# Moving a third of a transform stage: fewer half transforms beside a sort, more in its drain, twelve behind it

## The chip, the cores and the metric

The kernel runs on one core of one Trainium2 chip. The metric is the time on the device in microseconds, the median of the runs shown. Engines are called by the names in the profile: PE (TensorE, with PEld for its weight loads), DVE (VectorE), ACT (ScalarE), POOL (GpSimd) and SP (SyncE, which here only issues DMAs).

## The reference, cut to what matters

Eight sequences of 5,696 tokens with 128 channels are convolved along time with one long filter per channel, and the result goes through a mixture of eight experts, of which each token takes the one with the highest gate.

```python
Xf = np.fft.rfft(x, n=2 * S, axis=1)              # x: (8, 5696, 128)
Hf = np.fft.rfft(h, n=2 * S, axis=0)
y = np.fft.irfft(Xf * Hf[None], n=2 * S, axis=1)[:, :S, :]
t = y.reshape(B * S, D)
logits = t @ w_gate                                # (45568, 8)
e = argmax(logits); g = softmax(logits)[e]
out = g * (np.maximum(t @ w1[e], 0) @ w2[e])       # w1: 128x1024, w2: 1024x128
```

## The kernel before, in words

The long convolution is done as a transform of two factors. The eight sequences are three groups of 2, 3 and 3. A group passes three stages. **Phase a** (`steps_a`) cuts the sequence into items: `xt` (120 x 512 floats) is loaded, cut into a rounded part and a remainder (`xc`, one cast on ACT and one subtraction), and two *half transforms* `pa` are made of it (cosine and sine, three matmuls of 512 columns each), copied into `ut` (the cosine half by ACT, the sine half by DVE) and, when three items have filled a `ut`, stored to U in DRAM. The second group (g = 1) has 36 items, so 72 half transforms and 24 stores of 737 KB. **Phase b** (`phase_b`) takes 120 *48-point items*: `uq` holds four of them, read from all rows of U; `xp` is the forward matmul, DVE multiplies by the filter (`zt`, `xs`), a *combine* adds the two, and `vp` is the inverse matmul. Since `uq` reads every row block of U, its load waits for the last U store. **Phase c** (`phase_c`) is the sort: synthesis `yp`, a transpose `tp`, gate scores `gb`, then small operations on DVE (`route`, `rank`) that give each token its place, and POOL scatters the rows to SR by those positions, six scatters per unit of six blocks. After a group's sort, `tables` computes on DVE, in pieces, which expert each tile of 256 rows belongs to.

**The experts** (`experts`) load the weights `wb` and the rows `xr` of a tile, turn the rows (`mx`), and run two layers (`mh`, `ma`) of 24 matmuls each. A tile's `xr` waits for all scatters of its sort, and its `wb` for the tables, whose values SP reads into registers.

What runs beside what is settled when the program is built. `run` mixes several streams by a virtual clock: each stream yields a cost, which is divided by its share, and the one that is furthest behind goes next. All engines then work through their own queue in that order. While the first sort runs (space "c"), the second group's phase a and the cutting of the weights go beside it. Then the space "sb" is opened, and `run((experts(), 1.0), (back, SHARES[3]))` mixes the experts with `rest()`, which runs phases b and c of the second and third groups. The experts yield `None` and stand still until their part is *ready*; `begin(pt)` makes it so, after the rest of the tables' pieces are issued. In `rest()` two pieces are dealt out per 48-point item, and `begin` comes when more than `HEAD[g]` of cost has been spent, 5500 for the second group, at 704 per item.

A `Guest` is a phase a that is stepped by hand inside another stage; the third group's runs so within the second sort.

SP's queue is one list in order. Every DMA on it waits for the semaphore lane of the DMA eight places ahead, so at most eight are under way.

Of the kernel before, what the change touches and what calls it, by code (L numbers as in the profile page):

```python
# [13 lines left out]
F32 = mybir.dt.float32  # L14
F32R = mybir.dt.float32r
# [11 lines left out]
MP = 120  # L27
# [10 lines left out]
SIX = 4  # L38
MT = 4
# [6 lines left out]
F3 = (False, False, True, False)  # L46
MIX = 2
LD = 4
SHARES = (0.42, 0.195, 0, 0.75, 0.998, 0.42)
GAP = 5000  # L50
AHEAD = 2
ALONE = (0, 14, 10)
HEAD = (0, 5500, 9000)
A3 = (True, True, True, True)
ALO = ('gpsimd', 'vector', 'vector', 'vector')
AT = 650
# [15 lines left out]
def conv_moe(ctx: ExitStack, tc: tile.TileContext, I, out, B, S, D, E, F, split):  # L72
    nc = tc.nc
    P = 128
# [14 lines left out]
    ps = pool("ps", 2, PSUM)  # L89
# [15 lines left out]
    sb = Space()  # L105
# [6 lines left out]
    class Part:  # L112
        def __init__(self, gr, s, b0, nb, c0, tiles):
            self.gr, self.g, self.s, self.b0, self.nb, self.c0 = gr, gr.g, s, b0, nb, c0
            self.cols = nb * D
            self.ni = SLOTS[gr.g] // nb
            while NB % self.ni:
                self.ni -= 1
            self.ns = self.ni * nb
            self.cb = 3 if self.ns % 3 == 0 else 2  # L120
            self.cw = self.cb * D
            self.c3 = C3[gr.g]
            self.nt = tiles
            self.ready = False
            self.ends = []
            self.sets = 2 if b0 + nb == B else 1
# [138 lines left out]
        while late:  # L265
            nc.sync.dma_start(*late.pop(0))

    def steps_a(gr, tag, bufs):
        g, nb = gr.g, gr.nb
        srcs = [(I["x"][gr.b0 + b], b) for b in range(nb)]  # L270
        tw = 4 * D
        items = []
        for ig in range(NB // 4):
            for src, b in srcs:
                items.append((ig, src, b))
        xts, uts, xss = {}, {}, {}
        fore = (4, 3, 2)[g]
        split = A3[g]

        def cut(n):  # L280
            if not split or n >= len(items):
                return
            xt = xts.pop(n)
            xs = sb.tile([MP, 2, tw], F32R, tag="us", name=f"xc{g}_{n}", bufs=3 if g else 2)
            nc.scalar.copy(xs[:, 0], xt)
            getattr(nc, ALO[g]).tensor_tensor(out=xs[:, 1], in0=xt, in1=xs[:, 0].bitcast(F32), op=ALU.subtract)  # L286
            xss[n] = xs

        def load(n):
            if n >= len(items):  # L290
                return
            ig, src, b = items[n]
            xts[n] = sb.tile([MP, tw], F32, tag="xt", name=f"xt{g}_{n}", bufs=1 + fore)
            nc.sync.dma_start(xts[n], src[:, ig * tw : (ig + 1) * tw])

        banks, late = {}, []

        def flush():
            while late:
                nc.sync.dma_start(*late.pop(0))  # L300

        def transform(m):
            n, c = divmod(m, 2)
            banks[m] = ps.tile([P, 512], F32, tag="cx", name=f"pa{g}_{n}_{c}", bufs=4)
            ops = [(fcs[:, c], xts[n])] if not split else [(fcr[:, u, c], xss[n][:, v]) for u, v in PASSES]
            for k, (lhs, rhs) in enumerate(ops):
                mm(banks[m][:QN, :], lhs, rhs, start=(k == 0), stop=(k == len(ops) - 1))
            if c == 1:
                (xss if split else xts).pop(n)

        def store(m):
            n, c = divmod(m, 2)
            ig, src, b = items[n]
            if b == 0:
                uts[c] = sb.tile([QN, 4, gr.cols], F32, tag=tag, name=f"ut{g}_{ig}_{c}", bufs=bufs)
            srcv = banks.pop(m)[:QN, :].rearrange("p (i d) -> p i d", d=D)
            lo = c * NB + ig * 4
            cp = nc.scalar.copy if c == 0 else nc.vector.tensor_copy
            cp(uts[c][:, :, b * D : (b + 1) * D], srcv)  # L319
            if b == nb - 1:  # L320
                late.append((gr.U[:, lo : lo + 4, :], uts[c]))

        def start():
            for n in range(fore):
                load(n)

        def begin(m):
            if m == 0:
                cut(0)
            if m % 2 == 0:  # L330
                load(m // 2 + fore)
                cut(m // 2 + 1)
            transform(m)

        return start, begin, store, flush, 2 * len(items)

    def phase_a(gr):
        start, begin, store, flush, M = steps_a(gr, "six", SIX - gr.g)
        half = AT if gr.g == 0 else 750 * RATE[3 * gr.g - 3]
        start()  # L340
        for m in range(M + 2):
            if m < M:
                begin(m)
            if gr.g == 0 and m == M - 8:
                ahead_of_b()
            yield half
            flush()
            if 1 <= m <= M:
                store(m - 1)
        yield 0  # L350
        flush()

    class Guest:
        def __init__(self, gr):
            self.start, self.step, self.store, self.flush, self.M = steps_a(gr, "mt", MT)
            self.gr, self.m, self.open = gr, 0, []

        def begin(self, count):
# [367 lines left out]
    def phase_c(pt, guest=None):  # L726
# [202 lines left out]
        for n in range(n_end + 1):  # L929
            for k in range(nsub):  # L930
                at = n * nsub + k
                if k == (1 if n == 0 else 0):
                    load(n + 2)
                if n < nu:
                    synth(n, k)
                if TL <= at < total_sub + TL:
                    tp = ps.tile([P, 512], F32, tag=ytag, name=f"tp{g}_{n}_{k}", bufs=ybuf)
                    turn(*divmod(at - TL, nsub), tp)
                if k == nsub - 1 and n >= 1:
                    score(n - 1, n - 2 if g else None)  # L940
                if k == 0 and n >= (n_end if g else 2):
                    if g:
                        yield STEP
                    score(None, n - 2)
                lift(at + 2)
                if guest:
                    guest.begin(1 if k == nsub - 1 and n >= 1 else 2)
                yield cost if n < nu or pt is parts[-1] else cost / 2
                if guest:
                    guest.end()  # L950
                if n < nu:
                    divide(*divmod(at + AHEAD, nsub))
                    settle(n, k)
                lifted(at + 2)
                if 0 <= at - TL < total_sub:
                    turned(*divmod(at - TL, nsub))
                chains = []
                if g and k == nsub - 1 and 0 <= n - 2 < nu:
                    chains.append(rank(n - 2))
                if k == nsub - 1 and 0 <= n - 1 < nu:  # L960
                    chains.append(route(n - 1))
                if k == 0 and n >= (n_end if g else 2):
                    chains.append(rank(n - 2))
                zipped(*chains)
                if n == n_end:
                    break
# [346 lines left out]
    def chain(*gens):  # L1313
        for x in gens:
            yield from x

    def rest():
        wait = [groups[0].parts[-1]]
        for gr in groups[1:]:
            spent = 0  # L1320
            guest = Guest(groups[gr.g + 1]) if gr.g + 1 < len(groups) else None
            bins = phase_b(gr)
            for n, cost in enumerate(bins):
                if guest and n == QN * gr.nch - 12:
                    guest.start()
                spent += cost
                yield cost
                if wait:
                    for _ in range(2):
                        next(wait[0].pieces, None)  # L1330
                    if spent > HEAD[gr.g]:
                        begin(wait.pop())
            for pt in gr.parts:
                yield from gather(pt, guest)
            if guest:
                yield from guest.rest()
                wait.append(gr.parts[-1])
# [26 lines left out]
    with tc.manual_schedule():  # L1364
        prep = weights()
        back = rest()
        run((phase_a(g0), 1.0), (phase_h(), SHARES[4]), (consts(), 1.0))
        sb.close()
        sb.open("b")
        state["rests"] = True  # L1370
        run((phase_b(g0), 1.0), (prep, SHARES[0]), stop=(prep,))
        sb.close()
        sb.open("c")
        state["rests"] = False
        run((chain(*[gather(pt) for pt in g0.parts]), 1.0), (phase_a(groups[1]), SHARES[1]), (prep, SHARES[5]))
        sb.close()
        sb.close()
        sb.open("sb")
        run((experts(), 1.0), (back, SHARES[3]))
        sb.close()  # L1380
# [78 lines left out]
```

## Time and profile before

| what | value |
|---|---|
| median of 3 runs | 2154.88 us (2150.51 to 2156.96) |
| the profiled execution's own time | 2172.09 us |
| its span, first to last instruction | 2170.2 us |
| mean granted TensorE clock | 0.981 |
| PE busy | 2082.0 us, 96% |
| DVE, POOL, ACT busy | 1543.0, 1351.6, 1187.0 us |
| phase c of the first group, roughly | 226 to 398 us |
| HBM read and written | 571 and 154 MB |

Busy time of PE counts matmuls that are running, at whichever clock is granted, so a stretch can be busy and slow. The span is that of one execution; the time shown for a run lies some 2 us above its span. Windows are in us from the span's start.

### The profile page before, as it was taken

Reading aid. Unit: us, or ns where it says so; the run is one execution under the profiler, and the core shown is the slowest. Engines: PE = TensorE matmul, PEld = TensorE weight load, DVE = VectorE, ACT = ScalarE, POOL = GpSimd, SP = SyncE. Lnnn points to the kernel's source line nnn. Section 1 sums busy time; section 2 is a strip of 40 time slices with the busy share of each in tenths; the row PEclk is TensorE's granted clock in tenths of the full one; section 3 lists DMA queues with packets and bytes.
Section 4 is the critical chain, followed back from the end, with each engine's and each line's share of the span. In section 5 each row is a group of like instructions: output and inputs, shape, how many; then the busy total and the mean of one; then the engine's idle time right before and its main releaser. Section 6 shows DMA issues by size and latency. Waiting matters only on the chain.

```text
span 2170.2 us, 47112 instructions
## 1 busy us (share of the span) xinstructions
PE 2082.0 (96%) x14452; PEld 1858.2 (86%) x14452; DVE 1543.0 (71%) x3373; ACT 1187.0 (55%) x2429; POOL 1351.6 (62%) x1569
## 2 busy tenths in 40 slices
PE   9999999799999999989999999999998999999998
PEld 7799777377777888878888889999988999999998
DVE  4698667799997777788888887666665555555554
ACT  5677555255555665636666665555544444445444
POOL 6566387545554488887997785288883444444333
PEclk9999999699999999999999999999999999999999
DMA  8899798989986898858777865656533334444331
GB/s 267 263 292 286 233 289 269 248 211 236 242 243 181 226 274 247 251 158 223 191 184 203 213 180 152 150 129 154 135 95 96 95 128 134 132 131 128 121 120 36
DMA packets 213409, 409.32 MB, mean 189 GB/s; under 512 B 31605, under 2 KB 135339, under 8 KB 213156
## 3 DMA queue, kind: packets, MB, share of 16 engines
q1 hardware_dynamic: 184975, 350.70, 57.7%
q0 software_dynamic: 27072, 55.35, 8.9%
q8 instruction: 117, 1.92, 0.4%
q14 instruction: 136, 1.11, 0.2%
q10 hardware_dynamic: 1109, 0.23, 0.1%
HBM read 571.44 MB, written 154.27 MB: 334 GB/s over the span
## 4 chain that ended last, share of the span: by engine, by line
PE 81%; DMA 6%; DVE 5%; issue 4%; POOL 2%; ACT 2%; SPq 1%; another core or an unknown queue 0%; POOLq 0%; ACTq 0%; DVEq 0%
PE mh L167 22%; PE ma L167 22%; PE vp L167 9%; PE xp L167 8%; PE yp L167 5%; PE mx L191 4%; PE pa L167 4%; PE gb L167 2%; DMA mt<-mq 2%; PE tp L191 1%; DMA wb<-WD 1%; DMA xt<-x 1%; PE lb L191 1%; PE hp L167 1%; POOL xc L286 1%
## 5 line engine op out<-in xcount | busy, mean ns | idle before, releaser
L1183 DVE SCALAR_TENSOR_TENSOR hs<-mh,hs 128x512 fp32r<-128x512 f32 x728 | 501.7, 690 | 393.5 <-ACT hs L1181 297.0
L167 PE MATMUL mh<-xtb,wb 128*128 128x256 f32 x4368 | 703.9, 297 | 20.9 <-DVE hs L1183 6.1
L1181 ACT ACTIVATE hs<-mh 128x512 fp32r<-128x512 f32 x728 | 435.4, 598 | 482.1 <-PE mh L167 375.0
L167 PEld LDWEIGHTS mh<-xtb,wb 128*128 128x128 f32 x4368 | 586.7, 190 | 91.0 <-issue 35.3
L167 PE MATMUL ma<-hs,wb 128*128 128x256 f32 x4368 | 656.4, 287 | 2.4 <-DMA wb<-WD 2.4
L167 PEld LDWEIGHTS ma<-hs,wb 128*128 128x128 f32 x4368 | 572.7, 191 | 3.8 <-DMA wb<-WD 3.3
L676 POOL DMA_INDIRECT SR<-rt,pi x384 | 408.5, 1064 | 206.1 <-ACT xtb L1165 85.4
L694 POOL DMA_INDIRECT out<-xr x308 | 302.7, 983 | 348.0 <-ACT hs L1181 160.7
L573 POOL TENSOR_TENSOR zt<-zt,xs 128x384 f32<-128x384 f32 (+1 forms) x276 | 295.8, 1074 | 154.7 <-DVE xs L563 72.7
L567 DVE TENSOR_TENSOR xs<-xp,hh 64x384 f32<-64x384 f32 (+1 forms) x360 | 214.8, 597 | 7.8
L610 ACT COPY vt<-vp 96x384 f32<-96x384 f32 x240 | 114.0, 475 | 191.7 <-PE vp L167 168.5
L167 PE MATMUL vp<-zt,mi 128*96 128x384 f32 x480 | 198.9, 496 | 1.7 <-issue 1.0
L558 DVE TENSOR_TENSOR zt<-xp,hh 128x384 f32<-128x384 f32 (+1 forms) x300 | 173.5, 578 | 24.9 <-PE xp L167 17.5
L167 PE MATMUL xp<-uq,mt 96*128 96x384 f32 (+1 forms) x496 | 174.7, 456 | 8.3 <-DMA uq<-U 4.4
L167 PE MATMUL pa<-xc,fcr 120*120 120x512 f32 x576 | 161.9, 416 | 4.2 <-DVE ut L319 1.2
L563 DVE SCALAR_TENSOR_TENSOR xs<-xp,hh 64x384 f32<-64x384 f32 x240 | 134.3, 560 | 4.2
L906 POOL MEMSET spent<- 120x288 f32 (+1 forms) x366 | 127.4, 348 | 0.5
L167 PEld LDWEIGHTS pa<-xc,fcr 120*120 120x120 f32 x576 | 101.1, 189 | 28.8 <-DVE rk L895 2.2
L167 PE MATMUL yp<-vr,gcr 120*120 120x384 f32 x576 | 118.8, 341 | 6.1 <-ACT ut L319 4.4
L167 PEld LDWEIGHTS vp<-zt,mi 128*96 128x96 f32 x480 | 78.9, 166 | 50.6 <-issue 27.1
L319 DVE COPY ut<-pa 120x512 f32<-120x512 f32 x96 | 65.7, 684 | 73.1 <-PE pa L167 47.9
L167 PEld LDWEIGHTS xp<-uq,mt 96*128 96x128 f32 x496 | 87.1, 199 | 32.5 <-issue 15.8
(165 smaller groups left out, 2754.6 us busy)
## 6 DMA issues: line engine op xcount, KB each, us to landing
wb<-WD SPq DMA_DIRECT2D x728, 512.0 KB
U<-ut SPq DMA_DIRECT2D x48, 720.0 KB
uq<-U SPq DMA_DIRECT2D x60, 576.0 KB
V<-vt SPq DMA_DIRECT2D x60, 576.0 KB
vq<-V SPq DMA_DIRECT2D x48, 720.0 KB
xt<-x SPq DMA_DIRECT2D x96, 240.0 KB
xr<-SR SPq DMA_DIRECT2D x154, 130.0 KB
WD<-wsp SPq DMA_DIRECT2D x32, 512.0 KB
```

Source lines behind the costliest of these rows:

```text
L167: nc.tensor.matmul(to, lhs, rhs, **kw)
L191: nc.tensor.transpose(dst, src, ident[:n, :n])
L558: nc.vector.tensor_tensor(out=zt, in0=x3, in1=hv[:, 0].broadcast_to([P, PK, cb, D]), op=ALU.mult)
L563: nc.vector.scalar_tensor_tensor(out=xs[to, 0], in0=x3[at, 0], scalar=-1.0, in1=him[:, 0], op0=ALU.mult, op1=ALU.mult)
L567: nc.vector.tensor_tensor(out=xs[to], in0=x3[at], in1=him, op=ALU.mult)
L573: eng.tensor_tensor(out=zt, in0=zt, in1=xs, op=ALU.add)
L610: done = nc.scalar.copy(outs_[qb][:, k0 : k0 + PK, c * cw : (c + 1) * cw], banks.pop(n)[:K2, :iw].rearrange("p (q x) -> p q x", q=PK),)
L676: s = nc.gpsimd.indirect_dma_start(out=SR[:, :], out_offset=IndirectOffsetOnAxis(ap=pi[:, b : b + 1], axis=0), in_=rt[:, b, :], in_offset= ...
L694: sc = nc.gpsimd.indirect_dma_start(out=out[:, :], out_offset=IndirectOffsetOnAxis(ap=xr[:, s, D + 1 : D + 2].bitcast(I32), axis=0), in_=x ...
L906: nc.gpsimd.memset(spent.rearrange("p c q -> p (c q)")[:, : REST[g]], 0.0)
L1181: done = nc.scalar.activation(hs[:, 0], hp, AF.Relu)
L1183: done = nc.vector.scalar_tensor_tensor(out=hs[:, 1], in0=hp, scalar=0.0, in1=hs[:, 0].bitcast(F32), op0=ALU.max, op1=ALU.subtract)
```

## The change

Five numbers and three pieces of code change. `SHARES[1]` falls from 0.195 to 0.132, so fewer half transforms go beside each step of the first sort. In the sort's drain (`n >= nu`, the steps after its last synthesis) the yielded cost is now twice a step's instead of half, so more go there. `phase_a(groups[1], LATE)` ends after 30 items; the last six items, twelve half transforms, become a `Guest` named `late` at the head of `rest()`, behind the first sort and in front of the second group's phase b, with two pieces of the tables dealt out at each of its steps. `HEAD[1]` becomes 0, so `begin` follows the first 48-point item, and with it the experts are let go there. `ALONE[1]` falls from 14 to 2: the combine of items 2 to 13 moves from DVE to POOL.

```diff
+LATE = 30
-SHARES = (0.42, 0.195, 0, 0.75, 0.998, 0.42)
+SHARES = (0.42, 0.132, 0, 0.75, 0.998, 0.42)
-ALONE = (0, 14, 10)
-HEAD = (0, 5500, 9000)
+ALONE = (0, 2, 10)
+HEAD = (0, 0, 9000)
...
-    def steps_a(gr, tag, bufs):
+    def steps_a(gr, tag, bufs, lo=0, hi=None, fore=None):
...
+        items = items[lo:hi]
...
-        fore = (4, 3, 2)[g]
+        fore = fore or (4, 3, 2)[g]
...
-    def phase_a(gr):
-        start, begin, store, flush, M = steps_a(gr, "six", SIX - gr.g)
+    def phase_a(gr, hi=None):
+        start, begin, store, flush, M = steps_a(gr, "six", SIX - gr.g, 0, hi)
...
-        def __init__(self, gr):
-            self.start, self.step, self.store, self.flush, self.M = steps_a(gr, "mt", MT)
+        def __init__(self, gr, lo=0):
+            self.start, self.step, self.store, self.flush, self.M = steps_a(gr, "mt", MT, lo, None, 2)
...
-                yield cost if n < nu or pt is parts[-1] else cost / 2
+                yield cost if n < nu or pt is parts[-1] else cost * (0.5 if g else 2)
...
         wait = [groups[0].parts[-1]]
+        late = Guest(groups[1], LATE)
+        late.start()
+        for cost in late.rest():
+            for _ in range(2):
+                next(wait[0].pieces, None)
+            yield cost
...
-        run((chain(*[gather(pt) for pt in g0.parts]), 1.0), (phase_a(groups[1]), SHARES[1]), (prep, SHARES[5]))
+        run((chain(*[gather(pt) for pt in g0.parts]), 1.0), (phase_a(groups[1], LATE), SHARES[1]), (prep, SHARES[5]))
```

What this does to PE's queue at the end of the first sort: `yp0_15_1` is the sort's last synthesis, `gb0_15` its last gate scores, `pa1_n_c` half c of item n of the second group, and `xp1_0` the first 48-point item. Before:

```order
L167 MATMUL yp0_15_1_4577<-hh1_109,spent_78 120x384 x2
L191 MATMUL tp0_15_1_4580<-ident_87,rt0_15_4540 128x120 x3
L167 MATMUL gb0_14_None_4584<-c_moe_w_gate_93,yt0_14_4511 120x8 x6
L191 MATMUL tp0_16_0_4610<-ident_87,rt0_15_4540 128x120 x3
...
L167 MATMUL gb0_15_None_4651<-c_moe_w_gate_93,yt0_15_4593 120x8 x6
...
L167 MATMUL xp1_0_0_4724<-uq1_0_4710,mt1_0_4708 128x384
```

Of the change:

```order
L168 MATMUL yp0_15_1_4420<-hh1_109,spent_78 120x384 x2
L192 MATMUL tp0_15_1_4423<-ident_87,rt0_15_4383 128x120 x3
L168 MATMUL gb0_14_None_4427<-c_moe_w_gate_93,yt0_14_4337 120x8 x6
L168 MATMUL pa1_26_0_4440<-xc1_26_4369,fcr_84 120x512 x3
...
L168 MATMUL pa1_26_1_4471<-xc1_26_4369,fcr_84 120x512 x3
L168 MATMUL pa1_27_0_4479<-xc1_27_4437,fcr_84 120x512 x3
...
L168 MATMUL gb0_15_None_4533<-c_moe_w_gate_93,yt0_15_4446 120x8 x6
L168 MATMUL pa1_28_1_4542<-xc1_28_4476,fcr_84 120x512 x3
L168 MATMUL pa1_29_0_4547<-xc1_29_4492,fcr_84 120x512 x3
L168 MATMUL pa1_29_1_4552<-xc1_29_4492,fcr_84 120x512 x3
...
L168 MATMUL pa1_30_0_4622<-xc1_30_4614,fcr_84 120x512 x3
...
L168 MATMUL pa1_35_1_4734<-xc1_35_4711,fcr_84 120x512 x3
L168 MATMUL xp1_0_0_4770<-uq1_0_4756,mt1_0_4754 128x384
```

Before, all 72 half transforms stood ahead of `yp0_15_1`; now 52 do, eight stand between it and the sort's end, and twelve (`pa1_30_0` to `pa1_35_1`) between the sort and `xp1_0`.

Further on in PE's queue, the first tile of the experts: `mxNone_0` turns its rows and `mh0_0` is its first matmul group. Before:

```order
L167 MATMUL xp1_9_0_4919<-uq1_8_4768,mt1_8_4735 128x384
L167 MATMUL vp1_5_0_4921<-zt1_5_0_4831,mi1_112 96x384
L167 MATMUL xp1_10_0_4931<-uq1_8_4768,mt1_8_4735 128x384
L167 MATMUL vp1_6_0_4933<-zt1_6_0_4848,mi1_112 96x384
L191 MATMUL mxNone_0_4953<-ident_87,xr0_4892 128x128 x2
L167 MATMUL mh0_0_4959<-xtb0_4956,wb0_0_0_4875 128x256 x6
```

Of the change:

```order
L168 MATMUL xp1_0_0_4770<-uq1_0_4756,mt1_0_4754 128x384
L168 MATMUL xp1_1_0_4774<-uq1_0_4756,mt1_0_4754 128x384
L168 MATMUL xp1_2_0_4831<-uq1_0_4756,mt1_0_4754 128x384
L168 MATMUL xp1_3_0_4844<-uq1_0_4756,mt1_0_4754 128x384
L192 MATMUL mxNone_0_4863<-ident_87,xr0_4807 128x128 x2
L168 MATMUL mh0_0_4869<-xtb0_4866,wb0_0_0_4790 128x256 x6
L168 MATMUL xp1_4_0_4876<-uq1_4_4764,mt1_4_4762 128x384
L168 MATMUL vp1_0_0_4878<-zt1_0_0_4777,mi0_111 96x384
```

Before, 11 `xp` and 7 `vp` were ahead of `mh0_0`; now 4 `xp` are. The experts stay about that much further ahead of the second and third groups' stages down to the last sort.

SP's queue over the same change of stage, from the last U stores to the first tile's rows `xr0`. Before:

```order
L300 DMA U1_72<-ut1_11_0_4378 120x1536
L300 DMA U1_72<-ut1_11_1_4425 120x1536
...
L461 DMA mt1_0_4708<-mq 96x512
L475 DMA uq1_0_4710<-U1_72 96x4x384
...
L475 DMA uq1_4_4718<-U1_72 96x4x384
...
L461 DMA mt1_8_4735<-mq 96x512
L475 DMA uq1_8_4768<-U1_72 96x4x384
...
L1144 DMA wb0_0_0_4875<-WD_77 128x1024
...
L1116 DMA xr0_4892<-SR_69 128x260
```

Of the change:

```order
L302 DMA U1_72<-ut1_9_1_4540 120x1536
L296 DMA xt1_30_4610<-x 120x512
...
L296 DMA xt1_35_4689<-x 120x512
...
L302 DMA U1_72<-ut1_11_0_4707 120x1536
L302 DMA U1_72<-ut1_11_1_4709 120x1536
L463 DMA mt1_0_4754<-mq 96x512
L477 DMA uq1_0_4756<-U1_72 96x4x384
...
L477 DMA uq1_4_4764<-U1_72 96x4x384
...
L463 DMA mt1_8_4772<-mq 96x512
...
L1146 DMA wb0_0_0_4790<-WD_77 128x1024
...
L1118 DMA xr0_4807<-SR_69 128x260
```

The weights `wb0` and rows `xr0` have moved up, from behind four `uq` loads to behind two; the U stores of items 30 to 35 and their loads now stand between the first sort and `uq1_0`.

## Rows read from the trace of the kernel before

**Rows 1.** The page, part 2: TensorE in 40 slices.

```profile
PE   9999999799999999989999999999998999999998
```

**Rows 2.** Windows: length, busy us (x) of PE, PEld, DVE, ACT, POOL; PEclk, DMA.

```profile
226.00:370.00 144.00, 138.84 (x737) 107.48 (x736) 95.80 (x276) 80.07 (x175) 90.84 (x133) 0.95 0.87 267
...
390.00:400.00 10.00, 3.67 (x20) 2.94 (x19) 6.23 (x31) 0.94 (x3) 8.71 (x15) 0.66 1.00 251
400.00:410.00 10.00, 7.13 (x12) 2.97 (x12) 7.74 (x24) 0.47 (x1) 8.58 (x14) 0.67 1.07 255
...
420.00:430.00 10.00, 8.46 (x12) 3.43 (x13) 9.57 (x18) 1.30 (x3) 0.00 (x0) 0.50 1.00 339
...
490.00:540.00 50.00, 50.00 (x277) 37.30 (x276) 47.02 (x87) 26.24 (x55) 28.50 (x30) 1.00 0.90 234
```

**Rows 3.** Windows of two later changes of stage.

```profile
940.00:990.00 50.00, 41.11 (x239) 34.28 (x240) 45.90 (x111) 18.40 (x39) 37.40 (x46) 0.90 0.72 196
1590.00:1640.00 50.00, 41.02 (x308) 38.93 (x307) 29.08 (x99) 17.14 (x38) 34.89 (x50) 0.93 0.24 67
```

**Rows 4.** Scatters of the first sort on GpSimd: one tile, then groups.

```profile
L676 POOL DMA_INDIRECT SR<-rt,pi x96: 995/999/1502, 257.4 to 415.2; - x96
...
L676 POOL DMA_INDIRECT SR<-rt,pi x96 | 100.4, 1046 | 58.8 <-DVE wsp L258 27.7 <-issue 14.7 <-ACT xc L285 6.5
L906 POOL MEMSET spent<- 120x224 f32 x90 | 27.8, 309 | 0.1
```

**Rows 5.** Timeline, first expert tile: start, us, engine, operation [idle, releaser].

```profile
418.43 0.15 DVE L1066 TENSOR_TENSOR did<-did,nt 1x8 f32<-1x8 f32 x1
...
430.12 0.63 PE L191 MATMUL mxNone<-ident,xr 128*128 128x128 f32 x2
...
431.21 1.32 PE L167 MATMUL mh<-xtb,wb 128*128 128x256 f32 x6 [0.46 <-ACT xtb L1165]
```

**Rows 6.** Chain of work, first sort: start, us, what.

```profile
363.35 2.07 PE pa L167 x9
...
369.38 1.29 PE yp L167 x4
```

**Rows 7.** Timeline, a stall in the first sort, and its end.

```profile
348.75 2.78 PE L167 MATMUL yp<-hh,spent 120*120 120x384 f32 x4 [2.45 <-ACT rt L813]
...
386.80 1.53 PE L167 MATMUL yp<-hh,spent 120*120 120x384 f32 x4
...
397.52 0.25 DVE L901 TENSOR_REDUCE pi<-rk 120x6 int32<-120x54 f32 x1
...
398.98 5.08 PE L167 MATMUL xp<-uq,mt 96*128 96x384 f32 x8 [2.69 <-DMA uq<-U]
```

**Rows 8.** Groups of VectorE and ScalarE in the first sort.

```profile
L286 DVE TENSOR_TENSOR xc<-xt,xc 120x512 fp32r<-120x512 f32 x36 | 24.7, 689 | 19.4 <-ACT xc L285 18.6 <-issue 0.5
L319 DVE COPY ut<-pa 120x512 f32<-120x512 f32 x36 | 24.5, 680 | 12.4 <-PE pa L167 6.9 <-issue 3.0 <-DMA U<-ut 2.5
...
L285 ACT CAST xc<-xt 120x512 fp32r<-120x512 f32 x36 | 22.5, 628 | 0.0
```

**Rows 9.** Chain of work, the very first load.

```profile
2.13 3.97 DMA xt<-x
```

**Rows 10.** Timeline of SP's queue over the change of stage.

```profile
380.60 4.70 SPq L300 DMA_DIRECT2D U<-ut  x2
...
390.37 1.22 SPq L475 DMA_DIRECT2D uq<-U  x1
...
400.66 0.32 SPq L461 DMA_DIRECT2D mt<-mq  x1
...
418.77 1.98 SPq L1144 DMA_DIRECT2D wb<-WD  x4
```

**Rows 11.** DMA over 340 to 440 us, in 40 slices.

```profile
GB/s 345 276 308 292 295 286 99 241 170 250 267 326 143 265 322 224 144 238 149 289 344 191 253 215 250 256 229 285 223 234 283 61 318 357 361 319 273 146 255 136
```

**Rows 12.** Chain of work, 48-point items at full clock.

```profile
479.52 0.65 PE xp L167 x2
```

More of the change, by code (lines that the diff above doesn't have):

```diff
@@ L283, in cut @@
             xt = xts.pop(n)
-            xs = sb.tile([MP, 2, tw], F32R, tag="us", name=f"xc{g}_{n}", bufs=3 if g else 2)
+            xs = sb.tile([MP, 2, tw], F32R, tag="us", name=f"xc{g}_{lo + n}", bufs=3 if g else 2)
             nc.scalar.copy(xs[:, 0], xt)
@@ L292, in load @@
             ig, src, b = items[n]
-            xts[n] = sb.tile([MP, tw], F32, tag="xt", name=f"xt{g}_{n}", bufs=1 + fore)
+            xts[n] = sb.tile([MP, tw], F32, tag="xt", name=f"xt{g}_{lo + n}", bufs=1 + fore)
             nc.sync.dma_start(xts[n], src[:, ig * tw : (ig + 1) * tw])
@@ L303, in transform @@
             n, c = divmod(m, 2)
-            banks[m] = ps.tile([P, 512], F32, tag="cx", name=f"pa{g}_{n}_{c}", bufs=4)
+            banks[m] = ps.tile([P, 512], F32, tag="cx", name=f"pa{g}_{lo + n}_{c}", bufs=4)
             ops = [(fcs[:, c], xts[n])] if not split else [(fcr[:, u, c], xss[n][:, v]) for u, v in PASSES]
```

## The prediction

> **What bounds the kernel now.** I read the page's slices first. TensorE stands at 9 tenths nearly everywhere, with one hole, the eighth slice [rows 1]. The windows show it from 390 to 430 us: TensorE is busy 3.7 of 10 us, then 7 to 8.5, but with a granted clock of 0.66, 0.67 and 0.50, where 490 to 540 us shows 50.00 of 50 at 1.00 [rows 2]. 0.50 is the 1.2 GHz level. Ahead of the hole TensorE was busy 138.84 of 144 us. So after the hole this kernel costs what TensorE has to do, and a change here is worth the TensorE time that it wins or loses around this one change of stage. Two later changes of stage lose about 9 us each [rows 3]; the experts now run about one tile further ahead there, which I cost at nothing, because tile 37, the first of the second sort, still comes after that sort's release in the order. If that cover is gone it costs a part of those 9 us, either way.
>
> Three chains end in the hole. The scatters of the first sort leave GpSimd from 257.4 to 415.2 us [rows 4], though its own work for them is 100.4 + 27.8 us and 14.7 us between them, 143 in all. The tables are done at 418.6, because their pieces are dealt out two per 48-point item. Then the weights and rows are fetched, the first tile is turned at 430.12 and the first expert matmul starts at 431.21 [rows 5].
>
> **The change, part by part.** I follow one chain to that first expert matmul, as the order of SP's and TensorE's queues fixes it.
>
> Step 1, the main loop. Before the last synthesis of the first sort (yp0_15_1) the order now has 52 half transforms, where it had all 72. One takes 2.07/3 = 0.69 us [rows 6], and TensorE is nearly full there, so 20 x 0.69 = 13.8 us come off. The stall before 348.75 (2.45 us, and then matmuls at 2.78 us for 1.29, the low clock [rows 6, 7]) falls in a stretch whose transfer engines are busy 0.87 of the time; with fewer loads and stores I take 3 us more off (bounds 0 and 5). The last synthesis started at 386.80 [rows 7]; now 370.0.
>
> Step 2, the drain. From that start to the last positions (397.52 + 0.25) it took 11.0 us. Now four cuts and four copies of half transforms stand in VectorE's queue among the sort's small operations, at 0.689 and 0.680 us [rows 8], 5.5 us; VectorE waits there for TensorE in part, so I add 3.3 (bounds 0 and 5.5). The copy that the last U store of the shortened phase waits for stands one round of five small operations ahead of the end, 1.2 us: 370.0 + 11.0 + 3.3 - 1.2 = 383.1.
>
> Step 3, the first late load. xt1_30 stands in SP's queue behind that store; 0.7 us to issue. Its landing: the very first load of the kernel, with nothing beside it, took 3.97 us [rows 9]; the uq load behind other transfers took from 390.37 [rows 10] to 398.98 [rows 7], 8.6. Two to four U stores are in front of it, so I take 6.5, in the middle. With the ScalarE cut (0.63 [rows 8]): 390.9.
>
> Step 4, twelve late half transforms, six items. On VectorE an item takes 0.689 + 0.680 and its share of the tables. On TensorE it takes 1.4 us at full clock and, by the two yp rows, up to 3.0 at the low one; TensorE stands idle for some 10 us before, as in 390 to 400, where the clock was 0.66. I take 2.7 (bounds 2.0 and 3.0): 6 x 2.7 = 16.2, to 407.1. The tables' pieces come to their end in this stretch, so they no longer gate anything.
>
> Step 5, U back to SBUF. The two last U stores, 737 KB each by their shape, leave 1.2 us later (copy and issue). Before, the second of two stores was issued at 380.60 + 4.70 - 0.32 = 385.0 and the uq load that waits for it at 390.37 [rows 10]: 5.4 us for one. A second one adds 737 KB at about 290 GB/s, 2.5 us, of which I count 2.1: 7.5 (bounds 5.4 and 8). uq1_0 is issued at 407.1 + 1.2 + 7.5 = 415.8, where it was issued at 390.37.
>
> Step 6, from uq1_0 to the first tile. Behind uq1_0 SP's queue holds eleven loads, up to mt1_8, then four weight loads, then xr0. On TensorE the first tile's turn stands behind four 48-point items. Before, uq1_0 to mt1_8 took 10.3 us (390.37 to 400.66) and the weights to the turn 11.35 (418.77 [rows 10] to 430.12): 21.6 with the sort's scatters beside. By bytes it is 4.75 MB (two uq, two mt, four hh, four mi, four wb): at the 361 GB/s of the fullest slice [rows 11] 13.2 us and 1.5 for the first to start, 14.7. I take 18, since the scatters have gone by then. Turn at 433.8, first expert matmul 1.1 us later, at 434.9.
>
> Step 7, what TensorE still owes. Before, eleven xp and seven vp were done at the first expert matmul; now four xp. 7 + 7 pieces of two passes at 0.65 us [rows 12] are 9.1 us. Twelve combines move from VectorE to GpSimd: nothing, since the scatters end by about 401 (254 + 143 + a few waits) and GpSimd is free; with that cover gone each would wait up to 1.5 us behind a scatter.
>
> Sum: 434.9 - 431.2 + 9.1 = +12.8 us. The first tile comes seven items earlier in the order, but the transfers that it queues behind start 25 us later. The profiled execution has 2172.09 us of its own, 17.2 above the median of the runs shown; the sum, made against it, gives 2185, and carried to the median 2154.88 + 13 = 2168.
>
> The steps with transfers are where a rule of the Trainium skill bears. The one store of step 5 took 5.4 us for 737 KB and the uq load 8.6 us for 590 KB [rows 7, 10]. DMA: Bandwidth & Descriptors, section Anatomy of one DMA, gives about 2.0 us fixed and the bytes at 436 GB/s, which would be an estimated 3.7 and 3.4 us. By that page of the Trainium skill steps 5 and 6 would be 5.4 and 12.9 us instead of 7.5 and 18, and the sum an estimated +6; the trace's rows, with other traffic beside, do not agree, and I go by them. By the rule rival (a) would come true.
>
> **The rivals.** Measured differences below 0.3% (6.5 us) can't be told from none.
>
> (a) Hardly any change, 0.25. The hole empties the queues: nothing but this chain is moving, so the late load lands in 4.0 us, the stores take 6.6 and step 6 takes 14.7. That is 2.5 + 0.9 + 3.3 off: +6, 2161. For it: 357 and 361 GB/s in the stretch with only weights. Against it: U and uq move in pieces of 1.5 and 6 KB beside scatters, at 200 to 290.
>
> (b) Faster, 0.12. The end of the scatters sets the release, and it comes at about 401 instead of 416.2. With 4 us for the last one to land, 4 for the rows' load (the quiet load of step 3) and 1.1 for the turn, the first expert matmul is at 410: 410 - 431.2 + 9.1 = -12, 2143. It decides where uq1_0 is issued before 415.8 - 12.8 = 403. For it: of GpSimd's 58.8 us of waits 58.8 - 27.7 - 14.7 = 16.4 lie between the scatters of one unit and the next [rows 4], and a shorter loop removes them. Against it: SP's order, xr0 behind uq1_0, and twelve transforms that would have to end by 394, 11 us after the store in front of their first load.
>
> (c) The loop does not get shorter, 0.13. GpSimd needs 143 us for the scatters whatever TensorE does, and the loop's row buffers come free behind them; if that gives back half of step 1, 8.4 us, everything behind comes so much later: +21, 2176.
>
> The forecast itself has 0.50, with its own range +6 to +19, 2161 to 2174.
>
> **How the numbers follow.** Slower by over 0.3%: 0.50 and (c) 0.13, 0.63. Within: (a), 0.25. Faster: (b), 0.12. With the bounds all on the low side (2.0 us in step 1, 3.3, 2.5, 4.2, 2.1 and 3.3 in the five behind it) the sum is 17 us less, 2151; all on the high side (3.0, 2.2, 2.1, 1.8, 0.5, 3.6) it is 13 more, 2181. The range takes in (a) and (c), goes a little toward (b) and leaves the last two us: 2148 to 2179.
>
> **What would show it.** Right: the last yp of the first sort near 370; last scatter near 400; a hole with almost no TensorE work from about 380 to 391 and again from 408 to 420; late pa from 391 to 407 at a clock below 1; uq1_0 issued near 416; first mh near 435. Step 1 is wrong if the last yp is later than 376, step 4 if the late transforms take under 12 us, step 6 if turn follows uq1_0 within 14. The prediction fails if uq1_0 is issued before 406, or if the later changes of stage at 940 and 1590 shift by more than 5 us.

## The result, and the profile after

The changed kernel takes 2172.24 us (median of 5 runs, 2169.07 to 2177.52) where the kernel before takes 2154.88: a ratio of 1.0091, 95% interval 1.0075 to 1.0107, or 16 to 23 us more. The forecast was slower, 2168 us. The profiled execution of the changed kernel is its median run, with a span of 2170.4 us. That of the kernel before had a span of 2170.2 us, so those two traces end together and hide the difference; a second trace of the kernel before, with a span of 2152.0, is the first experiment below.

The page's line for TensorE, to be held against [rows 1]. The eighth slice, the hole, has fallen from 7 to 4.

```profile
PE   9999999499999999988999999999998999999998
```

Windows over the change of stage [rows 2]: length, busy us (x) of PE, PEld, DVE, ACT, POOL, then PEclk, DMA share, GB/s.

```profile
226.00:370.00 144.00, 141.79 (x810) 113.09 (x810) 100.32 (x314) 84.51 (x186) 104.48 (x156) 0.98 0.86 258
370.00:380.00 10.00, 5.33 (x25) 3.62 (x23) 6.48 (x22) 1.78 (x5) 8.71 (x14) 0.69 0.76 232
380.00:390.00 10.00, 3.55 (x8) 2.47 (x9) 2.77 (x8) 2.34 (x4) 8.88 (x13) 0.50 0.75 214
390.00:400.00 10.00, 8.04 (x30) 5.08 (x28) 9.52 (x29) 4.49 (x8) 7.50 (x8) 0.96 0.78 228
400.00:410.00 10.00, 0.00 (x0) 0.00 (x0) 1.61 (x11) 0.00 (x0) 0.00 (x0) 0.56 0.78 238
410.00:420.00 10.00, 5.46 (x8) 2.52 (x8) 5.38 (x10) 0.00 (x0) 0.00 (x0) 0.50 1.07 215
420.00:430.00 10.00, 1.74 (x5) 1.17 (x6) 1.77 (x5) 0.37 (x1) 1.29 (x1) 0.50 1.06 324
430.00:440.00 10.00, 10.00 (x37) 6.36 (x37) 7.73 (x15) 4.30 (x9) 3.99 (x4) 0.74 0.75 159
```

TensorE has two holes now: 370 to 390, before the first late load has landed, and 400 to 430, where for 10 us it does nothing at all. From 400 to 430 it is granted 0.50 to 0.56, the 1.2 GHz level, and it is back at 1.00 only behind 440. The timeline shows which transfers end the holes.

```profile
362.98 0.81 PE L168 MATMUL yp<-hh,spent 120*120 120x384 f32 x2
...
378.05 0.25 DVE L903 TENSOR_REDUCE pi<-rk 120x6 int32<-120x54 f32 x1
...
385.78 0.62 ACT L287 CAST xc<-xt 120x512 fp32r<-120x512 f32 x1 [10.07 <-DMA xt<-x]
...
386.45 0.78 PE L168 MATMUL pa<-xc,fcr 120*120 120x512 f32 x1 [9.92 <-ACT xc L287]
...
400.99 0.15 DVE L1068 TENSOR_TENSOR did<-did,nt 1x8 f32<-1x8 f32 x1
...
411.96 0.98 PE L168 MATMUL xp<-uq,mt 96*128 96x384 f32 x1 [12.48 <-DMA uq<-U]
...
427.80 0.69 PE L192 MATMUL mxNone<-ident,xr 128*128 128x128 f32 x2 [10.38 <-DMA xr<-SR]
...
428.95 1.04 PE L168 MATMUL mh<-xtb,wb 128*128 128x256 f32 x2 [0.46 <-ACT xtb L1167]
```

The tables are done at 401.0 and the last scatter leaves GpSimd at 398.2 (415.2 before, [rows 4]), yet the first tile is turned at 427.80. SP's queue shows what holds it: `wb` and `xr` stand behind the late loads, the last U stores and the loads of the first 48-point items.

```profile
377.53 13.82 SPq L296 DMA_DIRECT2D xt<-x  x6
393.23 8.86 SPq L302 DMA_DIRECT2D U<-ut  x4
402.13 0.95 SPq L463 DMA_DIRECT2D mt<-mq  x1
406.71 0.32 SPq L477 DMA_DIRECT2D uq<-U  x1
...
414.64 4.09 SPq L1146 DMA_DIRECT2D wb<-WD  x4
419.81 3.02 SPq L1118 DMA_DIRECT2D xr<-SR  x3
```

**TensorE's lost time.** All these kernels run the same matmuls, only in another order. So I gave every matmul a cost, the median distance from one start to the next of its kind over all the traces; the costs add up to 2017 us in each trace, and what a stretch takes beyond the costs of the matmuls that start in it is lost (idle, or at the low clock). The table has it by stretch, with the issue of `uq1_0` and the first expert matmul. The change in time is (ratio - 1) x 2154.88, with its interval; the ratio is to the kernel before as it was timed beside each.

| kernel | uq1_0 issued | first mh | lost 226 to 440 | lost behind 440 | change in time, us |
|---|---|---|---|---|---|
| before, trace shown ahead | 390.4 | 431.2 | 44.8 | 78.6 | |
| before_again | 387.5 | 428.1 | 41.0 | 63.3 | 0 |
| changed | 406.7 | 429.0 | 52.6 | 70.0 | +19.6 (16.2 to 23.1) |
| alone_14 | 404.9 | 427.2 | 51.5 | 71.6 | +21.1 (15.3 to 27.2) |
| no_late | 404.9 | 427.1 | 50.4 | 65.6 | +12.5 (8.0 to 16.8) |
| late_only | 405.5 | 437.3 | 51.4 | 63.9 | +14.4 (9.7 to 19.4) |
| release_only | 384.7 | 414.8 | 38.9 | 71.5 | +4.5 (0.9 to 8.4) |
| no_release | 402.8 | 433.7 | 49.2 | 65.9 | +10.1 (6.7 to 13.6) |
| share_drain | 401.0 | 434.5 | 49.8 | 65.6 | +9.7 (5.8 to 13.8) |
| share_0170 | 390.9 | 424.1 | 41.1 | 65.8 | -2.6 (-6.5 to 1.3) |
| rows_first | 409.9 | 412.9 | 41.7 | 61.4 | +0.2 (-3.7 to 3.9) |
| after_076 | 409.1 | 430.8 | 51.9 | 58.2 | +4.1 (0.0 to 8.0) |
| rows_first_076 | 408.3 | 412.0 | 42.4 | 61.5 | -0.4 (-3.9 to 3.2) |
| before_076 | 386.1 | 431.1 | 42.1 | 82.5 | +5.6 (0.4 to 10.6) |

Each kernel has one trace here but for before, whose two differ by 15 us behind 440. A column is to be read over several rows, not from one.

### The profile page after: what moved, and what is told of

Same layout as the page of the kernel before. It is cut to its first block, busy times and chain, and to the rows that moved or that the text cites. A ratio compares the mean times of both kernels' runs of the same rounds, so it can differ in the third digit from the quotient of the medians.

```text
span 2170.4 us, 47109 instructions
## 1 busy us (share of the span) xinstructions
PE 2069.4 (95%) x14452; PEld 1857.9 (86%) x14452; DVE 1535.4 (71%) x3361; ACT 1186.4 (55%) x2429; POOL 1359.1 (63%) x1581
## 4 chain that ended last, share of the span: by engine, by line
PE 82%; DMA 8%; DVE 4%; SPq 2%; issue 2%; POOL 1%; ACT 1%; POOLq 0%; ACTq 0%; DVEq 0%
PE mh L168 22%; PE ma L168 22%; PE vp L168 8%; PE xp L168 8%; PE yp L168 6%; PE pa L168 5%; PE mx L192 3%; PE gb L168 3%; DMA wb<-WD 2%; PE tp L192 2%; DMA mt<-mq 2%; DMA xt<-x 1%; PE lb L192 1%; PE gb_None L168 1%; PE hp L168 1%
## 5 line engine op out<-in xcount | busy, mean ns | idle before, releaser
L678 POOL DMA_INDIRECT SR<-rt,pi x384 | 403.5, 1051 | 185.2 <-issue 60.2
L575 POOL TENSOR_TENSOR zt<-zt,xs 128x384 f32<-128x384 f32 (+1 forms) x288 | 307.0, 1068 | 174.2 <-DVE xs L565 122.3
L762 DVE TENSOR_TENSOR vr<-vq,vr 120x768 fp32r<-120x768 f32 x96 | 91.5, 955 | 28.1 <-ACT vr L761 27.7
```

Of the source, the lines that this page charges most:

```text
L575: eng.tensor_tensor(out=zt, in0=zt, in1=xs, op=ALU.add)
L678: s = nc.gpsimd.indirect_dma_start(out=SR[:, :], out_offset=IndirectOffsetOnAxis(ap=pi[:, b : b + 1], axis=0), in_=rt[:, b, :], in_offset= ...
```

## The experiments

**A second execution of the kernel before.**

> The kernel before, unchanged, for a second profiled execution: the one shown took 2172.09 us, 17.2 above the median of its timed runs, so the two traces end together although the timed runs differ by 17.4. If that execution was late in one stretch (theory: somewhere ahead of the first expert matmul, since from 2100 us on both traces agree within 0.1 us while the stages between were up to 18 us apart), a second one ends near 2153 and shows first mh some 10 us or more ahead of 431.21. Rival: every profiled execution of this kernel is that late, and then it ends near 2170 again with mh at 431.

Its span is 2152.0 us. The end is as the theory had it, the place is not: its first mh stands only 3.1 us earlier. The rows are the tables' last step, the first mh, and the window behind it.

```profile
415.34 0.15 DVE L1066 TENSOR_TENSOR did<-did,nt 1x8 f32<-1x8 f32 x1
...
428.12 1.08 PE L167 MATMUL mh<-xtb,wb 128*128 128x256 f32 x4 [0.46 <-ACT xtb L1165]
```

```profile
430.00:440.00 10.00, 9.22 (x46) 6.09 (x45) 9.62 (x18) 5.47 (x11) 0.00 (x0) 1.00 0.85 202
```

From 226 to 440 us the first trace lost 3.8 us more than this one, and behind 440 us 15.3 more, of which 12.9 lie between 1400 and 1660. The page's excess of 17 us over the median was thus for the most part far behind the change of stage. From here on the second trace stands for the kernel before.

**The parts one by one.** `no_late` is the changed kernel without the Guest, `late_only` the kernel before with the Guest alone, `release_only` the kernel before with the earlier release alone.

```diff
# no_late, against the changed kernel
-LATE = 30
+LATE = 36
# late_only, against the changed kernel
-SHARES = (0.42, 0.132, 0, 0.75, 0.998, 0.42)
+SHARES = (0.42, 0.195, 0, 0.75, 0.998, 0.42)
-ALONE = (0, 2, 10)
-HEAD = (0, 0, 9000)
+ALONE = (0, 14, 10)
+HEAD = (0, 5500, 9000)
-                yield cost if n < nu or pt is parts[-1] else cost * (0.5 if g else 2)
+                yield cost if n < nu or pt is parts[-1] else cost * 0.5
# release_only, against the kernel before
-ALONE = (0, 14, 10)
-HEAD = (0, 5500, 9000)
+ALONE = (0, 2, 10)
+HEAD = (0, 0, 9000)
```

> The changed kernel with LATE 36: the last twelve half transforms run at the end of the first sort's space, in the same stream as the others, and no Guest stands at the head of the second part. Share 0.132, drain cost, HEAD 0 and ALONE 2 stay. Theory (the loss is the serial chain load, transforms, store, uq that begins only after the sort): the loads flow ahead, twelve half transforms take 8.3 us at full clock, so uq1_0 is issued some 12 us earlier than 406.71 and the time is 2157 to 2163. Rival (the early release of the experts or the combines on GpSimd cost the time): no gain, 2170 to 2175. Rival (the smaller share beside the sort is the loss): 2168 to 2175 too, but with the hole before the first xp gone.

> The kernel before with LATE 30 alone: share 0.195, drain cost a half, HEAD 5500 and ALONE 14 as before. 60 half transforms stand ahead of the last synthesis and twelve behind the sort. Theory (serial chain): the sort's loop is up to 8.3 us shorter, the chain behind it adds some 25, so 2163 to 2173. Rival (the share or the release is the loss): 2150 to 2158.

> The kernel before with HEAD 0 and ALONE 2 alone: the experts are let go at the first 48-point item, and the combine of items 2 to 13 goes to GpSimd. Four xp stand ahead of the first expert matmul where eleven xp and seven vp did. Theory (serial chain): no loss here, since the rows wait for the last scatter (415.2 us in the first trace) either way; the first mh 0 to 4 us earlier and 9.1 us of 48-point work owed, part of it filling later idle time: 2150 to 2162. Rival (the early release is the loss): 2166 to 2175.

They took 2165.95, 2167.45 and 2158.34 us, beside 2154.4 for the kernel before. `late_only` is where the theory put it. `no_late` gains 7 us on the changed kernel and not 9 to 15: without the Guest `uq1_0` is still issued at 404.93. Its queue shows why. The loads of the last items stand behind U stores that wait for their copies, and the stores end in one block.

```profile
377.79 5.01 SPq L302 DMA_DIRECT2D U<-ut  x2
382.86 2.28 SPq L296 DMA_DIRECT2D xt<-x  x2
385.23 12.22 SPq L302 DMA_DIRECT2D U<-ut  x4
397.54 1.98 SPq L463 DMA_DIRECT2D mt<-mq  x1
404.93 0.32 SPq L477 DMA_DIRECT2D uq<-U  x1
```

So in this stage it is not the Guest as such that is dear (50.4 us lost without it, 52.6 with it), but that the last U store comes 15 us or more later than in before_again (397.1 here, 381.7 there), in whichever stream the transforms run. The rest of the 7 us lies behind 440, where two traces of one kernel differ by more. `release_only` missed my first mh by 12 us: it stands at 414.78. The rows do wait for the last scatter there, but that one leaves at 409.0, and the tables are done at 399.7.

```profile
411.53 2.95 SPq L1116 DMA_DIRECT2D xr<-SR  x3
```

In before_again the last scatter left at 412.2, but the tables were done only at 415.34 (418.43 in the first trace, [rows 5]), and that held the first tile. The stage itself gains 2.1 us by the release, and the rest of the kernel loses 8.2.

**The other parts, and two other orders.** `no_release` is the changed kernel without the release, `share_drain` the kernel before with the share and the drain's cost alone, `share_0170` the same with a share that ends all half transforms inside the drain, and `rows_first` the changed kernel with the release ahead of the 48-point items.

```diff
# no_release, against the changed kernel
-ALONE = (0, 2, 10)
-HEAD = (0, 0, 9000)
+ALONE = (0, 14, 10)
+HEAD = (0, 5500, 9000)
# share_drain, against the changed kernel: the same two lines, and
-LATE = 30
+LATE = 36
# share_0170, against share_drain
-SHARES = (0.42, 0.132, 0, 0.75, 0.998, 0.42)
+SHARES = (0.42, 0.170, 0, 0.75, 0.998, 0.42)
# rows_first, against the changed kernel, in rest() behind the late Guest
+AHEAD_OF_B = 4000
...
             yield cost
+        begin(wait.pop())
+        yield AHEAD_OF_B
         for gr in groups[1:]:
```

> The changed kernel with HEAD 5500 and ALONE 14 put back; the late transforms, the share and the drain cost stay. In terms of TensorE time lost (length of a stretch less what its matmuls take at full clock) the changed kernel lost 52.5 us in 226 to 440 us and the kernel before, in its second execution, 40.9; behind 440 us it lost 6.6 us more, and the release alone, whose loss in 226 to 440 was 2.2 less than before, 7.2 more behind it. Theory A (the release runs the experts ahead of the other groups and that costs some 6 us at the later changes of stage): the loss behind 440 us comes back to that of before within 3 us, and the time is 2163 to 2167. Theory B (the differences behind 440 us are those between executions): the time stays at 2168 to 2176.

> The kernel before with share 0.132 and the doubled drain cost alone: 52 half transforms ahead of the last synthesis, 20 behind it in the same stream, no Guest, HEAD 5500, ALONE 14. Theory A (uq1_0 cannot be issued before the last of the 72 half transforms is stored, and those 20 end 15 us later than they did): first xp near 410 as in no_late (410.45), 2160 to 2166, nearly all of the loss of the changed kernel without its other parts. Rival (share and drain alone win, and it takes late or release to lose): 2148 to 2156.

> The changed kernel with the experts let go before the 48-point items: the release right behind the late transforms, so that the weights and rows of the first tile stand ahead of uq1_0 in SP's queue and its turn and two matmul groups ahead of the first xp in TensorE's. The tables are done at 401.0 and the last scatter leaves at 398.2 in the changed kernel, so nothing but the order keeps the first tile until 428.95. Theory (the order of SP's queue, weights and rows behind eleven loads that wait for the last U store, holds the first tile): wb issued at 402 to 406, first mh at 412 to 418, uq1_0 3 to 5 us later than 406.71, TensorE's loss in 400 to 440 some 8 us less, 2160 to 2166. Rival (transfers or the low clock bound the stretch whatever the order): first mh no earlier than 424, 2168 to 2176.

> The kernel before with share 0.170 and the doubled drain cost: 66 half transforms ahead of the last synthesis, six behind it and all of them ahead of the sort's last gate scores, none after it. HEAD 5500, ALONE 14, no Guest. Theory (what costs is that the last U store and with it uq1_0 come later; six half transforms fit into TensorE's waits in the drain): uq1_0 at most 2 us later than in before, the scatters some 4 us earlier, 2149 to 2155, no slower than before. Rival (any half transform moved behind the last synthesis delays uq by its full chain): 2157 to 2163.

They took 2162.16, 2161.28, 2153.29 and 2150.36 us, beside 2152.67. `share_drain` alone loses 9.7 us, and every kernel of the table that issues `uq1_0` behind 401 with the experts behind it loses 49 to 53 us in the stage. `share_0170` issues it at 390.86 and loses 41.1, as before does. First `share_drain`, then `share_0170`:

```profile
401.02 0.32 SPq L477 DMA_DIRECT2D uq<-U  x1
```

```profile
390.86 0.32 SPq L477 DMA_DIRECT2D uq<-U  x1
```

`no_release` is as its theory A had it: behind 440 it loses 65.9, within 3 us of before_again, where the changed kernel loses 70.0. The three parts do not add up (9.7 + 14.4 + 4.5 is 28.6, the whole is 19.6). The column of `uq1_0` fits that: the share alone and the Guest alone already move its issue by nearly as much as both.

`rows_first` shows the other half. Nothing of the late work is taken away and `uq1_0` is even later, but the weights and rows stand ahead of it.

```profile
402.28 2.26 SPq L1147 DMA_DIRECT2D wb<-WD  x4
405.63 3.72 SPq L1119 DMA_DIRECT2D xr<-SR  x4
409.41 0.42 SPq L464 DMA_DIRECT2D mt<-mq  x1
409.88 0.43 SPq L478 DMA_DIRECT2D uq<-U  x1
```

```profile
412.89 3.17 PE L169 MATMUL mh<-xtb,wb 128*128 128x256 f32 x12 [0.46 <-ACT xtb L1168]
416.90 0.88 PE L169 MATMUL xp<-uq,mt 96*128 96x384 f32 x2 [0.84 <-DMA uq<-U]
```

```profile
400.00:410.00 10.00, 0.00 (x0) 0.00 (x0) 0.00 (x0) 0.00 (x0) 0.00 (x0) 0.50 0.96 322
410.00:420.00 10.00, 6.95 (x33) 5.58 (x34) 2.60 (x5) 2.43 (x5) 0.00 (x0) 0.69 1.04 260
420.00:430.00 10.00, 8.18 (x49) 6.26 (x48) 9.68 (x18) 1.67 (x3) 2.21 (x2) 1.00 0.95 210
```

First mh at 412.89, 16 us earlier, 0.84 us of waiting for `uq` at the first 48-point item, the clock at 1.00 in the window from 420, and 10.9 us less lost in the stage than in the changed kernel. So the wait of 10.38 us before the turn at 427.80 was one of order; the idle stretch from 400 to 410 is still there. The release turns two queues round together, SP's and, for the same tile, TensorE's, and no run moved one without the other. The time is below the 2160 to 2166 of the theory: of the 19.4 us that `rows_first` gains on the changed kernel, 8.6 lie behind 440 (61.4 against 70.0), and no run shows why.

**The later stages.** With the release early, TensorE lost 18.5 to 21.4 us in 930 to 1000 and 11.6 to 13.4 in 1590 to 1660 (changed, `no_late`, `release_only`, `rows_first`, and `alone_14` below); with it late 16.3 to 18.2 and 8.9 to 10.0 (`before_again`, `late_only`, `no_release`, `share_drain`, `share_0170`). The first trace of before, with 18.6 and 14.9, does not fit the second pair. At the second change of stage SP's queue differs. `share_0170`, then `release_only`, from the last U store of the third group to its `uq2_0`:

```profile
924.07 1.15 SPq L302 DMA_DIRECT2D U<-ut  x2
929.09 0.80 SPq L1146 DMA_DIRECT2D wb<-WD  x2
929.93 0.33 SPq L463 DMA_DIRECT2D mt<-mq  x1
932.04 0.33 SPq L477 DMA_DIRECT2D uq<-U  x1
```

```profile
927.63 1.14 SPq L300 DMA_DIRECT2D U<-ut  x2
932.48 4.81 SPq L1144 DMA_DIRECT2D wb<-WD  x4
938.16 0.38 SPq L1116 DMA_DIRECT2D xr<-SR  x1
938.58 0.43 SPq L461 DMA_DIRECT2D mt<-mq  x1
939.44 0.33 SPq L475 DMA_DIRECT2D uq<-U  x1
```

Eight us there, 11.8 here, because a tile's weights and rows stand between. `after_076` and `rows_first_076` slow the experts against the other stages a little, by which SP's order at this place is that of before again; `before_076` does the same to the kernel before, as a control; `alone_14` puts only the combines back.

```diff
# after_076 and rows_first_076, against the changed kernel and rows_first
-SHARES = (0.42, 0.132, 0, 0.75, 0.998, 0.42)
+SHARES = (0.42, 0.132, 0, 0.76, 0.998, 0.42)
# before_076, against the kernel before
-SHARES = (0.42, 0.195, 0, 0.75, 0.998, 0.42)
+SHARES = (0.42, 0.195, 0, 0.76, 0.998, 0.42)
# alone_14, against the changed kernel
-ALONE = (0, 2, 10)
+ALONE = (0, 14, 10)
```

> The changed kernel with SHARES[3] 0.76 for 0.75: the second and third groups' stages go a little faster against the experts. In SP's queue at the second change of stage two weight loads then stand between the last U2 store and uq2_0, as in the kernel before, where the changed kernel has four and the rows xr35; the experts stand at tile 31.75 there (before 31.0, changed 32.25). In the five traces with HEAD 5500 TensorE lost 16.3 to 18.2 us in 930 to 1000 and 8.9 to 10.0 in 1590 to 1660 (the first trace of before left out), in the four with HEAD 0 or less 18.5 to 21.2 and 12.4 to 13.4. Theory (the earlier release costs later only by where the tiles' loads then stand in SP's queue): uq2_0 is issued some 8 us after the last U2 store, where it was 11.8 in release_only, and the two stretches lose some 3 to 5 us less in all, 2164 to 2169. Rival (the later loss has another cause): both stretches as in the changed kernel, 2169 to 2175.

> rows_first with SHARES[3] 0.76 for 0.75, for the same reason: two weight loads, and no rows, between the last U2 store and uq2_0. rows_first lost 21.1 us in 930 to 1000 and 13.4 in 1590 to 1660. Theory: some 3 to 6 us less there, 2147 to 2151, faster than both kernels. Rival (the later loss has another cause): 2151 to 2156.

> The changed kernel with ALONE 14 put back: the combines of items 2 to 13 go to VectorE again, all else as changed. Theory (GpSimd is free by 400 us, so the move costs and wins nothing): 2169 to 2175. Rival (the moved combines are a part of the loss, by delaying vp behind them): 2162 to 2168.

> The kernel before with SHARES[3] 0.76 for 0.75 alone. after_076 came out some 15 us below the changed kernel, more than the 3 to 5 that the expectation had given the two later changes of stage. Theory (0.76 takes back what the earlier release had shifted, so the gain belongs to the changed kernel alone): the kernel before is not faster by it, 2150 to 2158, with losses of TensorE behind 440 us of 62 to 70 us. Rival (0.76 is a better pace for the later stages whatever stands ahead of them): 2140 to 2148, and it would beat both kernels.

`after_076`, `rows_first_076` and `alone_14` took 2156.0, 2151.59 and 2174.17 us beside 2152.7; `before_076` took 2170.28 beside 2162.83 for the kernel before on the chip that it ran on. `alone_14` has the changed kernel's time (21.1 against 19.6, its interval 15.3 to 27.2): the combines cost nothing that can be told. `after_076` gains 15.5 us on the changed kernel (4.1 against 19.6), more than I had expected. In its queue `uq2_0` follows the last store by 8.5 us, as expected:

```profile
933.41 0.83 SPq L302 DMA_DIRECT2D U<-ut  x2
938.70 0.81 SPq L1146 DMA_DIRECT2D wb<-WD  x2
939.55 0.33 SPq L463 DMA_DIRECT2D mt<-mq  x1
941.89 0.34 SPq L477 DMA_DIRECT2D uq<-U  x1
```

But the stretch from 930 to 1000 still lost 20.0, because TensorE waited for that load nearly as long as in the changed kernel, 4.28 us (first row, `after_076`) and 4.57 (second row, changed), where `share_0170` waited 1.15 (third row):

```profile
946.97 1.62 PE L168 MATMUL xp<-uq,mt 96*128 96x384 f32 x2 [4.28 <-DMA uq<-U]
```

```profile
954.86 1.62 PE L168 MATMUL xp<-uq,mt 96*128 96x384 f32 x2 [4.57 <-DMA uq<-U]
```

```profile
937.37 0.88 PE L168 MATMUL xp<-uq,mt 96*128 96x384 f32 x2 [1.15 <-DMA uq<-U]
```

So the order of SP's queue is not the whole of the second change's loss: that theory fell there. What `after_076` won in its trace lies for the most part in the second sort (440 to 930: 13.7 lost against 18.4) and at the third change of stage (10.1 against 12.4). But the second sort's loss varies without an order that these parts would explain (`rows_first` 13.6, `rows_first_076` 20.0, `alone_14` 23.0), so where the 15.5 us come from is not shown. `rows_first_076` does not gain on `rows_first`; the two cures do not add. And `before_076` does not win, it is rather slower (82.5 lost behind 440, beyond the 62 to 70 of the theory; 34.5 of it in the second sort, where before_again lost 23.4, and 22.1 in 930 to 1000), so 0.76 is no better pace by itself. No kernel here beats the kernel before beyond what the measurement can tell.

## Why the prediction was right, and where its steps were off

The sum was +12.8 us for the stage and nothing behind it. Against the second trace of before the stage lost 11.6 us (52.6 against 41.0), and the rest 6.7 (70.0 against 63.3); with +0.0 ahead of 226 that is 18.3, and 18.4 is the difference of the spans. The direction and the stage were right. That 11.6 is so near to 12.8 is partly luck: the first mh was put 6 us too late, but against a trace that was itself 3.1 us late there, and 1.7 us of low clock behind it were left out.

What failed is the sentence on the two later changes of stage, "which I cost at nothing": its cover, tile 37 behind the second sort's release, was not what decides. In 930 to 1000 and 1590 to 1660 the changed kernel lost 1.4 and 2.5 us more than before_again, 3.9 of the 6.7; between the five kernels with the early release and the five traces with the late one named above, the means are 2.9 and 3.1 us apart. At the second change the record names the wait: for the load of the third group's first 48-point items TensorE stood idle 4.30 to 7.60 us in the five with the early release, and 0 to 2.04 in those with the late one, the first trace of before included. At the third the waits for the experts' weights `wb` hardly differ (5.4 to 7.5 us in all against 4.1 to 6.0), and the cause stays open. So does the reason why the load at the second change comes too late: `after_076`, with SP's order put back, still waited 4.28, and `before_076`, with the late release, 5.80. The release moves every later tile against the other stages, 1.25 tiles ahead in the order at the third group's first 48-point item, and the interleaving there is another; that this is the reason is argued and not shown, since no run held the lead of the experts and the order of the queue apart.

The other 2.8 of the 6.7 us are a balance of -5.0 in the second sort and +7.8 elsewhere; two traces of one kernel differ by 15.3 there. `release_only` (stage -2.1, behind it +8.2; 4.5 us slower as timed, 0.9 to 8.4) and `no_release` speak for a term of this size behind the stage, `rows_first` against it: it has the earliest release and only 61.4 behind 440.

Step by step, on the changed kernel's trace. **Step 1**, last synthesis 370.0: 362.98. The twenty half transforms were counted right, but the loop's own stalls were larger: from the first synthesis to the last it takes 129.6 us where before_again took 151.1, 21.5 less, of which 13.8 are the half transforms and 7.7 not my 3. **Step 2**, 13.1 us to the store: 14.1 (377.1). **Step 3**, 7.8 from the store to the first late half transform: 9.3, of which the load took 8.3 (377.53 to the cast at 385.78). **Step 4**, 17.4 with the last copy and issue: 15.6 (386.45 to 402.1). **Step 5**, 7.5: `uq1_0` follows at 406.71, 4.6, which is only just behind the 406 that the prediction had set as its limit. The estimate by the Trainium skill's DMA: Bandwidth & Descriptors, Anatomy of one DMA, was 5.4, nearer than mine; the fit in that section is for DMAs that GpSimd issues, and SP issues these, so its nearness here does not bear it out. **Step 6**, 18: 21.1 (406.71 to 427.80), with the transfer engines' share at 1.06 to 1.07 in the two windows from 410 to 430. By the same page of the Trainium skill it would have been an estimated 12.9, which the trace does not show. Rival (a), with 14.7 here and 4.0 for the late load of step 3, is refuted. **Step 7**, 9.1 us owed: first mh at 428.95 is 0.8 behind before_again, and 0.8 + 9.1 = 9.9 of the 11.6; the low clock, 0.74 in 430 to 440 where before_again had 1.00, fits the rest. The first mh came 6 us ahead of my 434.9: step 1's 7 us, while the others cancel but for 1.

Rival (c), a loop that does not get shorter, is refuted by step 1. Rival (b), the first tile at the end of the scatters and before's time regained, did not come true in the changed kernel for the reason named against it, SP's order with `xr0` behind `uq1_0`; `rows_first` turned that order round and took the 19 us back, 8.6 of them behind 440. My price for it, -12, was too good. In `rows_first` none of the eighteen 48-point pieces that stood ahead of the first mh in before is done there, 18 x 0.65 [rows 12] = 11.7 us owed: 412.9 - 428.1 + 11.7 = -3.5, and with what TensorE lost behind the first mh, at the low clock (0.69 in 410 to 420) and in waits, the stage came out at +0.7 (41.7 against 41.0).

## What to carry to other kernels

Work that is moved behind a stage is dear by the last store that the next stage waits for, not by its own length: here 12 to 20 half transforms of 0.69 us put behind the last synthesis cost the stage 8 to 12 us, because `uq1_0` could be issued only behind the last of them. Where one engine issues all loads in order, look at what is ready and stands behind something that waits: putting eight loads ahead of a waiting one took back what the change had lost, with the transforms left where they were. Moving six transforms instead of twenty (`share_0170`) did as well: it lost nothing to begin with. A program with a fixed interleaving answers a small shift with changes far behind it, so compare lost time by stretch over several variants, and do not cost "a tile earlier" at nothing.

## What the runs showed that I had not expected

Two executions of one program differed by 18.2 us in span (2170.2 and 2152.0), and 12.9 us of it lay in one stretch, 1400 to 1660, far from anything that was changed: one profiled execution is no measure of a change of 1%. And the low clock outlasted the wait that it followed: in the changed kernel TensorE was idle from 400 to 410, then 5.46 and 1.74 us of 10 busy at 0.50, and had 0.74 while it was busy for all of 430 to 440. In `rows_first`, with the same idle 10 us but 6.95 us of work in the next window, it had 0.69 there and 1.00 from 420.
